# Output stores on ScalarE's DMA queue, and a new written-out order, in a fused linear-attention and SoLU kernel

## The chip, the core and the metric

The kernel runs on one core of a Trainium2 chip. The time is the device time of one execution in microseconds (us); a figure for a kernel is the median of several runs. The core has five instruction streams that matter here: TensorE (PE, with its weight loads PEld), VectorE (DVE), ScalarE (ACT), GpSimd (POOL) and SyncE (SP), which only issues DMA transfers here. Each engine carries out its instructions in the order in which the program lists them for it, and waits where an input or a buffer is not ready.

## What is computed

Two steps, of which the second takes the result of the first as its 4608 x 512 input (8 batches, 8 heads, 576 tokens of 64):

```python
def phi(x):
    proj = np.einsum('bhsd,df->bhsf', x, w_phi)
    proj = proj - np.max(np.abs(proj), axis=-1, keepdims=True)
    return np.concatenate([np.exp(proj), np.exp(-proj)], axis=-1)
q_p, k_p = (phi(q), phi(k))
kv = np.einsum('bhsf,bhsd->bhfd', k_p, v)
z = np.sum(k_p, axis=2)
num = np.einsum('bhsf,bhfd->bhsd', q_p, kv)
den = np.einsum('bhsf,bhf->bhs', q_p, z)[..., None] + 1e-06
x = (num / den)                       # to 4608 x 512
h = x @ w_in                          # 512 -> 1024
e = np.exp(h - h_max)
solu = h * e / (np.sum(e, axis=-1, keepdims=True) + 1e-09)
ln = (solu - mu) / np.sqrt(var + 1e-06) * g_ln
return (ln @ w_out)                   # 1024 -> 512
```

## The kernel before

**Attention units.** The 64 heads are worked in 16 units of four heads, each in two halves of two heads. Of a unit, PE projects keys and queries (`pjk`, `pjq`, and `pjm` for the 64 tokens in the middle that do not fill a tile of 128); DVE takes the row maxima (`m`) and subtracts them (`dk`, `dq`); ACT forms the features with exponentials (`ek` of keys, `fq` of queries). PE sums features times values into `kvT`: over full tiles of tokens (`kvT<-ek,rawv`) and over the middle ones (`kvT<-ek,vz`); the sums of the key features go into the same bank, in the first units on PE from `ek` itself (`kvT<-ek,ones` and `kvT<-ek,ones_half`), later from sums that POOL made (`kvT<-zacc,ones`). `kvT` is evicted to `kvs` and turned into `kvf`. In the first two units PE turns it (`kvt<-ident,kvs`), and queries are turned there too (`dT<-ident,dq`, and `dqm` for the middle); from the third on both go through DRAM and back (`dk<-kvs`, `kvf<-dk`; `dqd<-dq`, `pT<-dqd`). Then PE makes `den` and `num` from `fq` and `kvf`, ACT evicts them (`dn`, `E`), and POOL puts the quotient together (`xa`, `xb`).

**Token tiles.** The 4608 rows are 36 tiles of 128 (t = 0 to 35). ACT and POOL split a tile into a high part and a remainder (`mxh`, `mxl`), PE multiplies by `w_in` (`h`, 24 matmuls of 512 columns: high by high, high by low, low by high), DVE takes the maximum `nm`, ACT the exponentials `eu`, DVE the product and the statistics; `ub`, `du`, `uTs` turn the product through DRAM, ACT and POOL split it (`uhs`, `uls`), and PE multiplies by `w_out` (`o`, again 24). ACT evicts `o` times the row factor `sc` to `os` (128 x 512, 256 KB), and a transfer `out<-os` stores it. The last tile is cut into two halves of 256 columns, with 24 matmuls of 256 columns, an eviction and a store of 128 KB for each.

**The order.** Each step is an `op` with a name, an engine and a function. `SEQUENCE` is a table with the 2458 steps by number, and the program emits them in that order; since the instructions are kept in program order on their engine, the table is the order of each engine. It also decides which slot of a pool a tile gets, since freed slots are given out again in that order. The columns `cost` and `prio` of an `op` decide nothing here. In the weights' preparation at the start, `wraw` (loaded weights scaled in place), `win_h`, `w_out_h` (the high parts) and `w<-w,gcol` (weights times `g_ln`) run on ACT between the features. Nearly all instructions are recorded at one line, that of the helper that keeps the order (L260 before).

All transfers of the kernel before, the 37 stores too, are issued by SP.

Of the kernel before, what the change touches and what calls it, by code (L numbers as in the profile page):

```python
# [16 lines left out]
DM, DF = 512, 1024  # L17
# [38 lines left out]
    2, 123, 1, 124, 125, 78, 127, 126, 313, 94, 87, 85, 129, 80, 81, 95, 128, 82, 83, 99, 96, 84, 98, 136, 97,  # L56
    135, 101, 102, 138, 141, 103, 142, 104, 10, 79, 89, 130, 90, 314, 100, 92, 91, 131, 105, 86, 173, 224, 88,
    218, 4, 133, 112, 315, 132, 134, 317, 106, 107, 113, 114, 139, 108, 174, 93, 175, 11, 115, 219, 137, 316,
    110, 12, 178, 116, 109, 111, 117, 143, 222, 189, 181, 180, 182, 33, 140, 5, 118, 154, 13, 179, 318, 220,
    176, 6, 199, 119, 157, 145, 14, 120, 121, 221, 223, 156, 155, 148, 160, 190, 15, 149, 177, 162, 159, 184,  # L60
    28, 38, 150, 284, 22, 275, 122, 158, 161, 197, 34, 200, 183, 198, 191, 194, 192, 187, 193, 7, 195, 201, 225,
    164, 185, 144, 202, 167, 146, 35, 186, 226, 188, 196, 8, 227, 228, 39, 163, 205, 206, 29, 165, 147, 166,
    203, 207, 43, 285, 168, 422, 36, 3, 169, 289, 40, 286, 30, 23, 208, 288, 41, 287, 209, 249, 31, 290, 230,
    204, 213, 214, 232, 233, 236, 231, 255, 44, 381, 252, 210, 268, 151, 372, 235, 215, 234, 296, 24, 229, 291,
    251, 211, 45, 9, 46, 276, 25, 216, 212, 270, 423, 152, 254, 217, 237, 238, 32, 37, 271, 250, 240, 273, 424,
    272, 278, 153, 243, 274, 416, 277, 239, 256, 257, 253, 269, 170, 171, 244, 426, 16, 425, 259, 258, 319, 245,
    241, 42, 292, 262, 48, 49, 365, 246, 172, 279, 297, 50, 325, 427, 263, 260, 449, 242, 294, 382, 47, 264,
    320, 261, 280, 386, 417, 295, 293, 247, 326, 26, 281, 282, 265, 17, 266, 418, 283, 485, 469, 520, 51, 476,
    450, 27, 248, 419, 383, 302, 327, 420, 52, 300, 18, 303, 388, 385, 384, 323, 19, 298, 299, 53, 304, 367,
    321, 301, 267, 368, 305, 421, 369, 387, 308, 20, 21, 1808, 309, 389, 306, 374, 307, 1844, 332, 1826, 334,  # L70
    1809, 521, 72, 322, 324, 486, 329, 60, 328, 1810, 1811, 66, 63, 373, 375, 390, 330, 393, 333, 331, 69, 67,
    522, 345, 428, 370, 310, 371, 593, 336, 394, 61, 524, 1845, 68, 523, 490, 1812, 335, 339, 492, 525, 1813,
    1814, 346, 429, 399, 75, 628, 376, 379, 340, 377, 62, 337, 338, 391, 584, 347, 471, 311, 366, 378, 474, 487,
    73, 1846, 312, 392, 348, 76, 349, 351, 352, 395, 472, 341, 430, 634, 451, 350, 380, 1847, 488, 1817, 491,
    489, 353, 64, 70, 397, 1848, 405, 355, 400, 57, 401, 71, 354, 65, 1827, 54, 1849, 398, 432, 1862, 357, 396,
    55, 532, 1850, 1853, 586, 533, 406, 434, 356, 407, 408, 1828, 1829, 435, 342, 470, 585, 433, 58, 359, 358,
    437, 497, 436, 409, 1854, 475, 410, 1815, 1851, 1830, 74, 431, 473, 493, 455, 498, 594, 629, 411, 439, 438,
    630, 595, 631, 598, 478, 1855, 597, 632, 494, 596, 600, 633, 402, 403, 56, 1831, 404, 412, 360, 599, 413,
    1832, 59, 503, 77, 440, 443, 457, 456, 452, 343, 534, 361, 1818, 1856, 495, 1863, 453, 539, 635, 536, 480,
    362, 363, 414, 496, 1864, 1857, 444, 344, 504, 1852, 477, 1835, 481, 577, 479, 415, 364, 505, 1865, 538,  # L80
    441, 1858, 640, 636, 1866, 483, 482, 1867, 537, 454, 1868, 1859, 509, 459, 1860, 1819, 499, 500, 442, 458,
    637, 638, 484, 1833, 510, 511, 460, 445, 526, 1871, 639, 1820, 698, 579, 512, 461, 540, 501, 506, 1821,
    1816, 535, 446, 690, 541, 462, 463, 502, 464, 580, 447, 705, 1861, 513, 527, 1822, 582, 1872, 1823, 465,
    528, 641, 448, 514, 515, 587, 466, 530, 1869, 529, 1870, 531, 507, 553, 467, 740, 554, 696, 508, 581, 583,
    605, 601, 602, 543, 542, 516, 1824, 606, 544, 611, 588, 468, 545, 517, 665, 1873, 518, 547, 603, 546, 1880,
    604, 741, 742, 697, 555, 589, 548, 744, 556, 1881, 706, 612, 591, 707, 613, 578, 746, 519, 1836, 590, 743,
    1882, 1883, 607, 558, 557, 559, 561, 549, 710, 745, 708, 712, 592, 709, 1884, 560, 562, 700, 566, 666, 703,
    563, 617, 564, 1885, 567, 618, 1886, 565, 569, 568, 619, 642, 817, 689, 550, 1837, 1898, 609, 1934, 610,
    608, 647, 852, 1874, 1935, 1875, 1834, 648, 649, 701, 1936, 620, 1887, 752, 571, 570, 1937, 1876, 1952, 702,
    621, 753, 711, 622, 704, 572, 1938, 1889, 1939, 644, 646, 721, 717, 718, 645, 1899, 1940, 691, 853, 856,  # L90
    650, 643, 614, 1877, 615, 722, 652, 616, 667, 551, 854, 1941, 552, 671, 1900, 1901, 653, 573, 692, 1943,
    1838, 694, 651, 855, 1902, 655, 574, 754, 654, 623, 858, 1878, 1903, 857, 693, 695, 1904, 624, 1953, 1839,
    719, 656, 747, 801, 808, 1890, 575, 668, 657, 713, 714, 625, 669, 803, 659, 748, 658, 1907, 672, 720, 715,
    716, 670, 806, 626, 818, 749, 804, 750, 660, 1825, 802, 627, 822, 819, 674, 821, 1954, 673, 1840, 1888,
    1942, 723, 576, 726, 727, 724, 725, 676, 824, 864, 820, 675, 805, 1841, 661, 1842, 677, 751, 729, 807, 823,
    825, 679, 826, 678, 756, 730, 964, 680, 1891, 731, 732, 827, 681, 683, 759, 761, 1892, 865, 662, 921, 1908,
    699, 663, 757, 810, 929, 733, 760, 859, 1909, 682, 1916, 860, 777, 684, 862, 1905, 965, 861, 758, 1910,
    1893, 1955, 1894, 829, 830, 828, 685, 734, 778, 1895, 920, 735, 686, 767, 762, 1956, 863, 966, 968, 763,
    728, 664, 835, 967, 969, 687, 1944, 809, 755, 1957, 1896, 766, 764, 930, 1958, 769, 812, 765, 1959, 1961,
    889, 815, 1897, 813, 1879, 779, 736, 768, 688, 1988, 780, 783, 2024, 782, 785, 771, 1041, 1843, 737, 1989,  # L100
    1911, 1962, 1026, 1990, 1991, 816, 931, 1960, 2025, 836, 738, 1992, 1993, 1912, 772, 1994, 1997, 814, 890,
    739, 1963, 932, 2006, 781, 1913, 2026, 2027, 841, 784, 934, 1970, 790, 791, 970, 1906, 1082, 1032, 1998,
    770, 773, 866, 774, 811, 831, 786, 1964, 913, 832, 788, 837, 936, 787, 1965, 935, 1914, 1995, 2028, 789,
    933, 842, 2007, 792, 843, 838, 2029, 871, 941, 793, 844, 833, 971, 873, 891, 834, 795, 2030, 868, 794, 915,
    839, 2008, 895, 1945, 2009, 1999, 896, 845, 942, 892, 870, 893, 869, 1966, 796, 840, 916, 976, 972, 2010,
    2033, 974, 918, 917, 973, 2011, 1917, 867, 1971, 1076, 1033, 922, 775, 846, 797, 1915, 874, 1967, 2034, 872,
    776, 924, 876, 919, 923, 798, 977, 878, 879, 847, 975, 2012, 877, 1001, 875, 881, 848, 937, 1968, 938, 927,
    880, 1077, 925, 928, 939, 883, 2000, 894, 940, 897, 947, 1042, 1972, 849, 1080, 1043, 850, 1078, 2001, 1996,
    1079, 945, 884, 2013, 1002, 914, 851, 978, 885, 1003, 2015, 1973, 948, 2002, 1025, 1046, 1045, 898, 900,
    1946, 946, 980, 882, 2003, 953, 1044, 799, 949, 1974, 902, 903, 1047, 1975, 1081, 926, 899, 1048, 901, 800,  # L110
    1947, 954, 955, 904, 1976, 982, 981, 2004, 905, 907, 1979, 1027, 886, 1188, 1083, 956, 2031, 957, 1086, 943,
    887, 906, 2035, 1028, 1088, 908, 983, 944, 985, 1084, 1030, 958, 1144, 1031, 1194, 1153, 888, 979, 1948,
    909, 1007, 1004, 1918, 1949, 1919, 984, 986, 2036, 987, 1029, 1085, 1087, 2005, 1980, 1089, 1034, 1008, 910,
    1950, 911, 991, 950, 951, 988, 1137, 1090, 990, 952, 2032, 1920, 989, 959, 1113, 1005, 1051, 992, 960, 1052,
    993, 1921, 961, 1922, 995, 912, 994, 2096, 1189, 1154, 1049, 1009, 1036, 1155, 1095, 1190, 1925, 1191, 2097,
    1114, 1923, 2078, 1192, 996, 2098, 2037, 1158, 1039, 962, 1147, 1926, 1156, 1159, 2099, 2038, 1053, 963,
    1146, 1969, 1927, 997, 2016, 1300, 1951, 1115, 998, 2039, 2100, 1050, 1165, 1006, 1097, 1010, 1193, 1065,
    1040, 2014, 1157, 1037, 1014, 2101, 1015, 1057, 1160, 1012, 1054, 2017, 2042, 1058, 1091, 1059, 1060, 2040,
# [1188 lines left out]
```

## Time and profile before

| | before |
|---|---|
| median of 3 runs | 663.02 us (662.71 to 663.58) |
| the profiled execution | 664.01 us |
| its span (first to last event of the core) | 662.2 us |
| PE busy | 653.7 us, 99% of the span |
| DVE, ACT, POOL busy | 495.1, 368.9, 409.1 us (75%, 56%, 62%) |
| granted TensorE clock | 1.00 (full) in every slice |
| DMA, mean over the span | 209 GB/s, 138.45 MB |

The profiled execution is 1.8 us longer than its span, and 0.99 us longer than the median. The number of a row of a timeline is its start in the span; a timeline's time in brackets is how long the engine had stood idle before that row, and what released it. A matmul row's end is modelled and reaches into the next row, so the time that a block of matmuls takes is read from one row's start to the next one's.

### The profile page before, as it was taken

The numbers are of one execution on the slowest core, as the hardware profiler recorded it, in microseconds if no ns is written. First come the engines' busy times: TensorE is split into PE (matmuls) and PEld (weight loads), VectorE is DVE, ScalarE is ACT, GpSimd is POOL, SyncE is SP. The second block draws the span as 40 slices with busy tenths as digits, with TensorE's granted clock in tenths as the row PEclk, the third lists the DMA queues.
The fourth block names the chain that finished last, engine by engine and source line by source line (L and its number), as shares of the span: only waits on it lengthen the run. The fifth ranks groups of instructions, "written<-read, shape, count | busy, mean of one in ns | idle before, by whom it ended". The sixth has DMA issues, their size and how long they took to land.

```text
span 662.2 us, 13124 instructions
## 1 busy us (share of the span) xinstructions
PE 653.7 (99%) x4900; PEld 490.5 (74%) x4900; DVE 495.1 (75%) x750; ACT 368.9 (56%) x713; POOL 409.1 (62%) x447
## 2 busy tenths in 40 slices
PE   8999999999999999999999999999999999999997
PEld 6766767668777777777777777877677877788886
DVE  6999987788978687799968879788679665355340
ACT  4997775466564744556565665355745464324221
POOL 0239998757866546667876575856654775455342
PEclk9999999999999999999999999999999999999999
DMA  8987787887487946887667856874786544424241
GB/s 269 346 270 237 221 251 210 270 259 214 134 265 255 296 151 182 272 260 230 201 197 230 287 151 176 266 227 124 229 282 199 191 149 120 123 110 162 112 167 72
DMA packets 133296, 138.45 MB, mean 209 GB/s; under 512 B 55664, under 2 KB 106736, under 8 KB 132720
## 3 DMA queue, kind: packets, MB, share of 16 engines
q1 hardware_dynamic: 133232, 137.61, 65.9%
q8 instruction: 39, 0.64, 0.4%
q14 instruction: 25, 0.20, 0.1%
HBM read 87.10 MB, written 50.48 MB: 208 GB/s over the span
## 4 chain that ended last, share of the span: by engine, by line
PE 87%; DVE 6%; DMA 4%; issue 1%; ACT 1%; SPq 0%; ACTq 0%
PE o L260 30%; PE h L260 29%; PE kvT L260 11%; PE num L260 6%; PE pjk L260 4%; PE pjq L260 4%; PE den L260 2%; DVE m L260 2%; DVE w L260 1%; DVE dq L260 1%; DMA rawq<-in_q 1%; DVE dk L260 1%; DMA pT<-dqd 1%; PE pjm L260 1%; DMA dk<-kvs 1%
## 5 line engine op out<-in xcount | busy, mean ns | idle before, releaser
L260 POOL TENSOR_TENSOR uls<-uTs,uhs 128x1024 fp32r<-128x1024 f32 x36 | 86.6, 2410 | 61.8 <-ACT uhs L260 47.6
L260 PE MATMUL o<-w_out_h,uhs 128*128 128x512 f32 (+1 forms) x296 | 114.6, 387 | 0.0
L260 ACT ACTIVATE ek<-dk 128x512 f32<-128x512 f32 (+1 forms) x160 | 89.7, 584 | 44.1 <-DVE dk L260 39.4
L260 PE MATMUL o<-w_out_l,uhs 128*128 128x512 f32 (+1 forms) x296 | 113.6, 384 | 0.0
L260 PE MATMUL o<-w_out_h,uls 128*128 128x512 f32 (+1 forms) x296 | 113.5, 383 | 0.0
L260 PE MATMUL h<-win_h,mxh 128*128 128x512 f32 x288 | 91.2, 398 | 0.3 <-DVE dq L260 0.3
L260 DVE TENSOR_REDUCE nm<-h 128x1 f32<-128x1024 f32 x36 | 43.9, 1218 | 62.9 <-PE h L260 62.9
L260 PE MATMUL h<-win_l,mxh 128*128 128x512 f32 x288 | 88.9, 390 | 0.0
L260 PE MATMUL h<-win_h,mxl 128*128 128x512 f32 x288 | 88.8, 389 | 0.0
L260 ACT ACTIVATE fq<-pT 128x512 f32<-128x512 f32 (+1 forms) x140 | 74.5, 559 | 21.4 <-DMA pT<-dqd 13.8
L260 POOL TENSOR_TENSOR zt<-ek 128x512 f32<-128x512 f32 x52 | 68.8, 1322 | 24.4 <-ACT ek L260 22.8
L260 ACT ACTIVATE eu<-h,nm 128x1024 f32<-128x1024 f32 x36 | 40.0, 1111 | 69.3 <-DVE nm L260 60.3
L260 PEld LDWEIGHTS o<-w_out_h,uhs 128*128 128x128 f32 x296 | 55.6, 188 | 13.4 <-issue 1.6
L260 PEld LDWEIGHTS o<-w_out_h,uls 128*128 128x128 f32 x296 | 55.6, 188 | 11.0
L260 PEld LDWEIGHTS o<-w_out_l,uhs 128*128 128x128 f32 x296 | 55.6, 188 | 10.6
L260 PEld LDWEIGHTS h<-win_h,mxh 128*128 128x128 f32 x288 | 52.4, 188 | 13.9 <-issue 1.1
L260 PEld LDWEIGHTS h<-win_l,mxh 128*128 128x128 f32 x288 | 54.0, 188 | 11.5
L260 PEld LDWEIGHTS h<-win_h,mxl 128*128 128x128 f32 x288 | 54.1, 188 | 11.5
L260 PE MATMUL kvT<-ek,rawv 128*64 128x256 f32 x512 | 61.9, 384 | 0.0
L260 POOL TENSOR_TENSOR xa<-E,rb 128x576 f32<-128x576 f32 (+1 forms) x32 | 29.7, 931 | 51.9 <-DMA rb<-d 40.7
L260 DVE TENSOR_TENSOR eu<-h,eu 128x1024 f32<-128x1024 f32 x36 | 43.6, 1212 | 17.9 <-ACT eu L260 17.7
L260 PE MATMUL num<-fq,kvf 128*64 128x448 f32 (+1 forms) x304 | 56.2, 500 | 0.0
(96 smaller groups left out, 1231.9 us busy)
## 6 DMA issues: line engine op xcount, KB each, us to landing
du<-ub SPq DMA_DIRECT2D x36, 512.0 KB, 3.7
uTs<-du SPq DMA_DIRECT2D x36, 512.0 KB, 4.9
rb<-d SPq DMA_DIRECT2D x64, 144.0 KB, 4.4
dqd<-dq SPq DMA_DIRECT2D x14, 640.0 KB, 4.3
pT<-dqd SPq DMA_DIRECT2D x14, 640.0 KB, 5.8
out<-os SPq DMA_DIRECT2D x35, 256.0 KB, 3.2
rawq<-in_q SPq DMA_DIRECT2D x32, 256.0 KB, 4.7
rawk<-in_k SPq DMA_DIRECT2D x32, 256.0 KB, 4.5
```

What stands on the lines that cost most here:

```text
L260: return self.tc.keep_in_program_order(method(*args, **kwargs))
```

## The change

The stores of the output are issued by ACT (`nc.scalar.dma_start`) instead of SP, in ACT's order of steps; all other transfers stay with SP. `SEQUENCE` is another order of the same 2458 steps. No other line differs.

```diff
 SEQUENCE = (
...
-    2, 123, 1, 124, 125, 78, 127, 126, 313, 94, 87, 85, 129, 80, 81, 95, 128, 82, 83, 99, 96, 84, 98, 136, 97,
...
-    2435, 2452, 2311, 2455, 2436, 2400, 2383, 2239, 2401, 2453, 2456, 2454, 2437, 2457, 2409, 2417, 2410, 2418,
-    2419,
...
+    2433, 2428, 2434, 2435, 2436, 2382, 2418, 2437, 2383, 2419, 2451, 2446, 2452, 2453, 2454, 2455, 2456, 2457,
 )
...
     def moe_od_last(t, half):
         cs = slice(half * 256, half * 256 + 256)
-        nc.sync.dma_start(out=out[t * P : (t + 1) * P, cs], in_=M["os", t][:, cs])
+        nc.scalar.dma_start(out=out[t * P : (t + 1) * P, cs], in_=M["os", t][:, cs])
...
     def moe_od(t):
-        nc.sync.dma_start(out=out[t * P : (t + 1) * P, :], in_=M["os", t])
+        nc.scalar.dma_start(out=out[t * P : (t + 1) * P, :], in_=M["os", t])
...
-            op(n("od", hf), "sync", dma(2 * P * DM), z + 18 + hf, moe_od_last, (t, hf), [n("oe", hf)], (), [n("os")])
+            op(n("od", hf), "scalar", dma(2 * P * DM), z + 18 + hf, moe_od_last, (t, hf), [n("oe", hf)], (), [n("os")])
...
-        op(n("od"), "sync", dma(4 * P * DM), z + 19, moe_od, (t,), [n("oe")], (), [n("os")])
+        op(n("od"), "scalar", dma(4 * P * DM), z + 19, moe_od, (t,), [n("oe")], (), [n("os")])
```

Three places of the order follow, as the built kernels have it. A row is the line of the program, the operation, the tiles (output<-inputs, without numbers), the shape, and how many of them follow each other.

**First place.** PE in the second unit, from the first half's sum over full tiles on. Before:

```order
L260 MATMUL kvT<-ek,rawv 64x256 x8
L260 MATMUL pjm<-wph,rawk 128x128 x2
L260 MATMUL pjm<-wph,rawq 128x128 x2
L260 MATMUL kvT<-ek,vz 64x256 x4
L260 MATMUL kvT<-ek,ones 32x128 x16
L260 MATMUL kvT<-ek,ones_half 32x128 x4
L260 MATMUL dT<-ident,dq 128x128 x8
L260 MATMUL kvT<-ek,rawv 64x256 x8
```

Now:

```order
L259 MATMUL kvT<-ek,rawv 64x256 x8
L259 MATMUL pjm<-wph,rawk 128x128 x2
L259 MATMUL pjm<-wph,rawq 128x128 x2
L259 MATMUL kvT<-ek,vz 64x256 x4
L259 MATMUL kvT<-ek,rawv 64x256 x8
L259 MATMUL kvT<-ek,ones 32x128 x16
L259 MATMUL kvT<-ek,ones_half 32x128 x4
```

The second half's sum over full tiles, which needs all four `ek` steps of that half's keys, has moved up to stand directly behind the middle tokens. The row sums and the turns of queries that stood between them come after it; one `dT<-ident,dq 128x128 x4` stands further ahead than before.

**Second place.** PE between the third and the fourth unit: `kvT` is the first half of the fourth, `den` belongs to the third. Before:

```order
L260 MATMUL kvT<-fq,kvf 64x128 x4
L260 MATMUL num<-fq,kvf 64x448 x4
L260 MATMUL kvT<-ek,vz 64x256 x4
L260 MATMUL den<-fq,kvf 32x288 x8
L260 MATMUL kvT<-zacc,ones 32x128 x4
```

Now:

```order
L259 MATMUL kvT<-fq,kvf 64x128 x4
L259 MATMUL num<-fq,kvf 64x448 x4
L259 MATMUL kvT<-ek,vz 64x256 x4
L259 MATMUL kvT<-zacc,ones 32x128 x4
L259 MATMUL den<-fq,kvf 32x288 x8
```

The last matmuls into `kvT` have changed places with `den`. Behind both orders stand the same rows up to the first that reads the turned sums: 24 matmuls `h`, `pjm`, `pjq`, and `kvT<-ek,rawv`. On DVE the step that evicts this `kvT` to `kvs` stood behind the turn `ub<-eu` of a token tile, and now stands ahead of it.

**Third place.** ACT at the end of the program. Here the rows name what an instruction waits for as well: a count of another engine (PE, DVE, Pool, Activation), or of one of the eight counters (DMAHW0 to 7) that the transfers use in turn. Before:

```order
L260 ACTIVATE eu,sm<-h,nm 128x1024 [waits DVE_49,Pool_49]
L260 CAST uhs<-uTs 128x1024 [waits DMAHW4_49]
L260 ACTIVATE os<-o,sc 128x512 [waits DMAHW1_49,PE_49,Activation_49]
L260 CAST uhs<-uTs 128x1024 [waits DMAHW6_49,Activation_49]
L260 ACTIVATE os<-o,sc 128x512 [waits PE_49,Pool_49]
L260 ACTIVATE os<-o,sc 128x512
L260 ACTIVATE os<-o,sc 128x256 [waits DMAHW7_49,PE_49,Activation_49]
L260 ACTIVATE os<-o,sc 128x256 [waits PE_49]
L260 ACTIVATE os<-o,sc 128x512 [waits DMAHW0_49,PE_49,Pool_49]
```

Now:

```order
L259 DMA out<-os 128x512 [waits DMAHW1_49,Activation_49]
L259 CAST uhs<-uTs 128x1024 [waits DMAHW0_49,Pool_49]
L259 ACTIVATE os<-o,sc 128x512 [waits PE_49,Pool_49]
L259 ACTIVATE os<-o,sc 128x512 [waits DMAHW2_49]
L259 ACTIVATE os<-o,sc 128x512 [waits DMAHW5_49]
L259 DMA out<-os 128x512 [waits Activation_49]
L259 DMA out<-os 128x512 [waits DMAHW3_49,Activation_49]
L259 DMA out<-os 128x512 [waits Activation_49]
L259 ACTIVATE os<-o,sc 128x256 [waits DMAHW6_49,PE_49,Pool_49]
L259 DMA out<-os 128x256 [waits Activation_49]
L259 ACTIVATE os<-o,sc 128x256 [waits PE_49]
L259 DMA out<-os 128x256 [waits Activation_49]
```

Before, a whole tile of 512 columns was evicted last; now the two halves of 256 columns come last. The stores stand among ACT's own instructions, and some of them wait for a counter of the transfers as SP's do: through the program 25 of the 37 do so. Such a counter's wait holds until the transfer that used that counter before, eight transfers earlier in the program, has landed.

## Rows read from the trace of the kernel before

**Rows 1.** Busy time of each engine by stretch: length, then engine, busy us (instructions), granted clock, DMA

```profile
0.00:100.00 100.00, 95.25 (x1096) 68.40 (x1098) 91.39 (x158) 77.08 (x153) 59.71 (x57) 1.00 0.84 266
100.00:658.00 558.00, 558.00 (x3807) 422.03 (x3804) 403.69 (x593) 291.14 (x560) 349.44 (x391) 1.00 0.64 200
```

**Rows 2.** Waits of PE, whole span: releaser, us in total, times, longest

```profile
PE kvT L260 <- DMA kvf<-dk: 1.3, 1, 1.3
PE pjm L260 <- DMA rawk<-in_k: 0.9, 2, 0.6
```

**Rows 3.** Waits of SP's DMA queue, whole span

```profile
SPq L260 <- DVE kvs L260: 95.5, 26, 9.3
...
SPq L260 <- ACT os L260: 34.1, 9, 8.9
```

**Rows 4.** Store instructions on SP: ns min/median/max, first and last start

```profile
L260 SPq DMA_DIRECT2D out<-os x37: 332/424/1848, 120.1 to 659.3; - x37
```

**Rows 5.** Chain that ended last, 149 to 169 us: start, us, what

```profile
149.45 5.67 PE h L260 x24
...
162.77 5.44 PE h L260 x24
```

**Rows 6.** Timeline of PE from 35 us: start, us, instructions, idle before and releaser

```profile
35.23 0.49 PE L260 MATMUL pjm<-wph,rawk 64*128 64x128 f32 x4 [0.36 <-DMA rawk<-in_k]
...
35.87 0.66 PE L260 MATMUL kvT<-ek,vz 64*64 64x256 f32 x8
36.46 1.08 PE L260 MATMUL kvT<-ek,ones 128*32 128x128 f32 x32
...
37.69 1.09 PE L260 MATMUL dT<-ident,dq 128*128 128x128 f32 x8
...
46.07 1.18 PE L260 MATMUL den<-fq,kvf 128*32 128x288 f32 x16
```

**Rows 7.** Timeline of ACT from 31 us

```profile
31.95 1.19 ACT L260 ACTIVATE wraw<-wraw 128x1024 f32<-128x1024 f32 x1
33.03 1.14 ACT L260 ACTIVATE ek<-dk 128x512 f32<-128x512 f32 x2
...
35.12 0.98 ACT L260 COPY E<-num 128x288 f32<-128x288 f32 x3
35.98 0.65 ACT L260 ACTIVATE ek<-dk 128x512 f32<-128x512 f32 x1
...
37.62 0.64 ACT L260 ACTIVATE ek<-dk 128x512 f32<-128x512 f32 x1
```

**Rows 8.** Timeline of ACT from 45 us

```profile
45.15 2.61 ACT L260 ACTIVATE w<-w,gcol 128x512 f32<-128x512 f32 x4
```

**Rows 9.** Timeline of DVE from 89 us

```profile
89.54 0.58 DVE L260 STREAM_TRANSPOSE kvs<-kvT 128x384 f32<-128x384 f32 x1 [0.73 <-ACT E L260]
```

**Rows 10.** Timeline of SP's DMA issues from 90 us

```profile
90.52 0.52 SPq L260 DMA_DIRECT2D du<-ub  x1
```

**Rows 11.** Chain that ended last, 90 to 104 us

```profile
90.15 5.31 DMA dk<-kvs
...
95.48 4.27 DMA kvf<-dk
...
102.31 0.97 PE den L260 x16
```

**Rows 12.** Timeline of ACT from 655 us

```profile
655.76 0.48 ACT L260 ACTIVATE os<-o,sc 128x256 f32<-128x256 f32 x1 [2.36 <-PE o L260]
658.56 0.69 ACT L260 ACTIVATE os<-o,sc 128x512 f32<-128x512 f32 x1 [2.32 <-PE o L260]
```

**Rows 13.** Landing of the last store, from the view of tile os

```profile
DMA to landing us min/median/max: 2.0/2.0/2.0
```

**Rows 14.** DMA issues: KB each, median us to landing

```profile
dk<-kvs SPq DMA_DIRECT2D x28, 192.0 KB, 2.4
...
out<-os SPq DMA_DIRECT2D x2, 128.0 KB, 1.7
```

251 rows, old and new, of the table SEQUENCE are left out of this document.

## The prediction

> **What bounds the kernel now.** I read the busy times by stretch first [rows 1]. PE is busy for 558.00 of the 558.00 us between 100 and 658 us; ahead of 100 us it is busy for 95.25 of 100, and behind 658 for almost nothing. So a change of the order can take out at most the 4.75 us of idle PE at the head, and some of the tail; everywhere else it can only shuffle work that lies beside PE, or add waits to it. The clock is 1.00 throughout, so nothing is to be had there. The waits of PE say what the idle time at the head is [rows 2]: one of 1.3 us for the turned sums `kvf` coming back from DRAM, and two of 0.9 us together for loads of keys. Last I read the waits of SP, since the stores leave it [rows 3]: SP waits 34.1 us for `os` in 9 stores, the longest 8.9, and all transfers behind those stores wait with it. But the first store starts at 120.1 us [rows 4], where PE has no idle time left to give back. Moving the stores can't help the head, and behind 100 us it can help nothing on PE.
>
> **The change part by part.** *PE's own work: 0.* The steps are the same ones. A block of 24 matmuls of 512 columns takes 5.44 us, and 5.67 where PE enters it from the smaller kinds [rows 5], so an order could cost 0.23 us for each further change of kind. Counted in both orders, there are 31 stretches of `h` and `o`, and 167 changes of kind; with the durations of the trace on each row both orders come to 648 us of pure work, 0.1 apart.
>
> *First place, second unit: +0.95.* Its key sum over the second half needs the last `ek` of the unit. Before, that `ek` starts at 37.62 and takes 0.64, so it is ready at 38.26 [rows 7], while the row sums and turns from 36.46 on keep PE at work [rows 6]. Now the sum stands directly behind the middle tokens. PE reaches it at 36.46, plus 0.52 for the four turns moved ahead (half of the 1.09 for eight), so at about 36.98; less 0.36 if the wait for keys at 35.23 is covered by them [rows 6]. ACT's list up to that `ek` has lost one `wraw`, 33.03 - 31.95 = 1.08, and one `E`, (35.98 - 35.12)/3 = 0.29, and gained one `fq` of about 0.53: ready at 38.26 - 0.84 = 37.42 [rows 7]. PE waits 0.44 more than before, whether as 0.44 here, or as 0.80 here and the 0.36 gone. If ACT keeps its old pace, without the 0.84, it waits 1.3; if earlier differences favour it, nothing: 0 to 1.3. The `den` that follows moves too: on ACT two `w<-w,gcol` of 0.65 each [rows 8] and one more `wraw` stand ahead of the `fq` that it needs, which came behind it or sooner; they use up ACT's spare time there. Walked along the same rows, the last `fq` of the second `den` comes at 47.7 and PE at 47.8, a tie that any delay of ACT turns into a wait. I take 0.5, between 0 and the 1.08 of the `wraw`.
>
> *Second place, fourth unit: -1.2.* The chain is `kvs` at 89.54 [rows 9], `dk<-kvs` from 90.15 for 5.31 us, `kvf<-dk` from 95.48 for 4.27 [rows 11]; it is late by 1.3 us [rows 2]. Now the last matmuls into this `kvT` run ahead of `den` instead of behind it, so 0.97 us earlier [rows 11], while the reader of `kvf` stays where it was. `kvs` waited 0.73 us with DVE idle [rows 9], and on DVE the 1.25-long `ub` that stood ahead of it now comes behind, so DVE is free in time; and `du<-ub`, 512 KB issued at 90.52, just behind `dk<-kvs` [rows 10], comes later and no longer shares the engines with it. The median landing of `dk<-kvs` is 2.4, not 5.31 [rows 14]. 0.97 for sure would leave 0.3; with a part of the 2.9 I take -1.2, bounds 0 (another load in its way) and -1.3.
>
> *The other waits of the head: -0.3.* The two waits for keys, 0.9 us together [rows 2], now have four turns or a projection ahead of them, but what sets them is when a load lands, which the order hardly moves. Bounds 0 and -0.9; a third, since only the later one, of 0.36, is clearly covered.
>
> *The tail: -0.4.* Before, the last thing evicted is a whole tile, 0.69 us, against 0.48 for a half [rows 12]; the last store lands 2.0 us after its start [rows 13], that of a half takes 1.7 in the median [rows 14]. Now halves come last: -0.2 and -0.3, of which I take -0.4; bounds -0.2 and -0.5. PE's last 24 matmuls of 256 columns take as long as 12 of 512.
>
> *The stores on ACT: +0.2.* 37 x 0.424 = 15.7 us of issuing [rows 4] goes from SP to ACT. ACT is busy for 291.14 of 558 us there [rows 1], so 267 us of idle time hide it. If that cover were gone, ACT would be a bound and PE would see up to 15.7; at 55% busy it is not near. What could show is a wait: 25 stores carry the counter of a transfer eight places earlier, and ACT, with `eu`, `E`, `fq` or `mxh` behind the store, stands until that has landed. Laying PE's durations along the order, that transfer's place is 5 to 20 us ahead of the store; SP reaches transfers late by up to 9.3 us where it waits for `kvs` [rows 3], so a hold of some us can happen, and PE is reached only if ACT's lead is used up. I take 0.2; bounds 0 and 2.6, two waits the size of the 1.3 in [rows 2].
>
> What SP gains from the move is seen in [rows 3]: 34.1 us of standing still for `os`, more than the 15.7 of issuing. The Trainium skill ("DMA: Bandwidth & Descriptors", section "Issuing engines are not separate DMA queues") says that transfers started by several engines run on the same 16 DMA engines, and that issuing from more of them saves only the sequencer's time. By that rule the move alone is worth nothing in time and the sum without its +0.2 would be -0.95, 662.1 us; the trace agrees in so far as SP's waits reach no PE wait behind 100 us, but shows 34.1 us, not 15.7, freed on SP.
>
> The sum: 0 + 0.45 + 0.5 - 1.2 - 0.3 - 0.4 + 0.2 = -0.75, against the profiled execution's 664.01: 663.3. That execution is 0.99 above the median of the runs shown, so against the median it is 663.02 - 0.8 = 662.2 us.
>
> **The rivals.** *Slower: ACT is held by a store.* One mechanism: a store on ACT waits for the transfer that used its counter, SP comes to that transfer late, and the `eu` or `fq` behind the store reaches PE late. For it: SP's waits of up to 9.3 us [rows 3], and places with only 5 to 7 us between the two. Against it: the usual distance is 10 us or more, and PE has had no wait behind 100 us though ACT itself stood idle for 267 us. It decides when SP's lateness plus the landing exceeds the distance by more than ACT's lead. At 1.3 us each, two such places turn -0.8 into +1.8: 664.8 us.
>
> *Faster: the new order doesn't delay the head.* If ACT, whose list is shorter at the first place, is ready in time, the +0.95 is gone, and the waits go as far as they can: -1.3 - 0.9 - 0.5 = -2.7, 660.3 us. For it: the place holds less `wraw` work ahead of the key sum; against it: PE now comes to that sum at 36.6 to 37.0, ahead of the 37.69 at which it still had turns to do before [rows 6], and ACT's 0.84 doesn't reach that far.
>
> *Nothing happens:* that the second place is hidden anyway can't be, its 1.3 us stand on PE; but it may be given back one step later, at the next sum of the unit, and then the forecast's -0.8 is about 0, 663.0 us. I count this inside the forecast.
>
> **How the numbers follow.** Forecast 0.48, its own range 661.2 to 663.6; slower rival 0.26; faster rival 0.26. A measurement of this kernel tells about 0.2%, 1.3 us, from no change: faster is below 661.7, slower above 664.35. Of the forecast a quarter lies below, 0.05 above; of the faster rival nine tenths below; of the slower one seven tenths above. Faster 0.12 + 0.23 = 0.35, slower 0.02 + 0.18 = 0.20, the rest, 0.45, within. The range runs from the faster rival's 660.3, a little below for its own spread, to a little above the slower rival's 664.8: 660.2 to 665.0.
>
> **What would show it.** PE's waits in the changed profile: the one for `kvf<-dk` near 100 us gone or below 0.4; a new one for ACT `ek` between 36 and 38 us, and one for `fq` ahead of `den` near 47; PE full again from 102 us to the last matmul; the last eviction a half of 0.48 us. Among SP's waits `os` is gone, and ACT shows waits for transfers in front of its stores. The prediction is wrong if PE is idle by more than 0.5 us anywhere between 100 and 650 us (the slower rival), or if PE's idle time ahead of 100 us falls below 3 us (the faster one).

## The result and the profile after

The changed kernel takes 667.33 us (median of 15 runs, 663.44 to 671.58), the kernel before 663.44 beside it (15 runs, 662.71 to 665.15): a ratio of 1.0061, 95% interval 1.0046 to 1.0076. It is slower by 0.6%, and its runs spread three times as wide. The forecast of 662.2, range to 665.0, was wrong, and no rival named what made it slower. The profiled execution took 667.28 us, with a span of 665.5.

The busy times of the changed kernel by stretch, the answer to [rows 1] (length; then PE, PEld, DVE, ACT, POOL; granted clock, DMA share, GB/s):

```profile
0.00:100.00 100.00, 97.28 (x1100) 70.87 (x1102) 88.72 (x152) 76.94 (x153) 59.24 (x56) 1.00 0.84 273
100.00:300.00 200.00, 200.00 (x1532) 147.68 (x1530) 164.38 (x256) 116.78 (x235) 137.63 (x155) 1.00 0.73 224
300.00:400.00 100.00, 99.56 (x736) 74.51 (x733) 84.47 (x127) 57.99 (x113) 65.11 (x68) 1.00 0.71 223
400.00:500.00 100.00, 96.28 (x699) 71.52 (x698) 84.26 (x118) 54.35 (x107) 63.51 (x67) 1.00 0.66 202
500.00:660.00 160.00, 160.00 (x828) 126.61 (x828) 78.79 (x102) 62.77 (x108) 84.52 (x104) 1.00 0.46 147
```

The head has less idle time than before (2.72 us against 4.75), but between 300 and 500 us PE now stands still for 0.44 + 3.72 us, where before it never did. PE's waits name the places, the answer to [rows 2]:

```profile
PE pjq L259 <- issue: 2.3, 1, 2.3
PE den L259 <- DVE qz L259: 1.5, 2, 1.0
...
PE dT L259 <- DVE dq L259: 0.7, 1, 0.7
PE dT L259 <- DVE dqm L259: 0.6, 1, 0.6
PE o L259 <- ACT E L259: 0.4, 1, 0.4
```

The waits for `kvf` and for keys are gone; `qz` is new. It is a step of the later units (from the second half of the fifth on): ACT and then DVE scale the query features by their sums, so that `den` is a plain sum over `qz`. The DVE step in the view of that tile, first before, then after: ns min/median/max, first and last start.

```profile
L260 DVE SCALAR_TENSOR_TENSOR qz<-fq,kvf,qz x46: 777/819/2733, 145.7 to 558.6; 128x576 f32<-128x576 f32 x46
```

```profile
L259 DVE SCALAR_TENSOR_TENSOR qz<-fq,kvf,qz x46: 771/819/6078, 143.2 to 565.5; 128x576 f32<-128x576 f32 x46
```

One instruction of the same shape takes 0.82 us or 6.08. The timelines of the changed kernel around it, DVE, POOL and PE, show when:

```profile
403.18 1.21 DVE L259 TENSOR_REDUCE nm<-h 128x1 f32<-128x1024 f32 x1
404.31 7.28 DVE L259 SCALAR_TENSOR_TENSOR qz<-fq,kvf,qz 128x576 f32<-128x576 f32 x2
411.52 1.27 DVE L259 BATCH_NORM_STATS2 bst<-eu 128x6 f32<-128x512 f32 x2
...
414.17 1.28 DVE L259 TENSOR_TENSOR dk<-pjk,m 128x512 f32<-128x512 f32 x2
```

```profile
403.42 1.28 POOL L259 TENSOR_TENSOR zacc<-zacc,ek 64x512 f32<-64x512 f32 x1
404.67 0.32 POOL L259 TENSOR_TENSOR xa<-E,rb 128x64 f32<-128x64 f32 x1
404.95 1.26 POOL L259 TENSOR_TENSOR xb<-E,rb 128x512 f32<-128x512 f32 x1
406.18 2.35 POOL L259 TENSOR_TENSOR uls<-uTs,uhs 128x1024 fp32r<-128x1024 f32 x1
408.50 1.27 POOL L259 TENSOR_TENSOR zt<-ek 128x512 f32<-128x512 f32 x1
409.85 1.13 POOL L259 TENSOR_TENSOR zacc<-zt 128x256 f32<-128x256 f32 x1
```

```profile
411.74 0.69 PE L259 MATMUL den<-qz,ones 128*32 128x288 f32 x8 [1.01 <-DVE qz L259]
412.23 0.43 PE L259 MATMUL kvT<-zacc,ones 128*32 128x128 f32 x8
414.96 1.16 PE L259 MATMUL pjq<-wph,rawq 64*128 64x128 f32 x16 [2.30 <-issue]
...
417.42 0.50 PE L259 MATMUL o<-w_out_h,uhs 128*128 128x512 f32 x1 [0.41 <-ACT E L259]
```

The rows show five POOL instructions without a gap from 403.42 to 409.77, and the first gap, 0.08 us, ahead of the second `zacc`, which has to wait for `zt`. The first of the two `qz` ends 0.62 us behind the start of that gap (6.08 us after 404.31, at 410.39), and the `zacc` that follows the gap is itself longer than usual (1.13 us; 0.74 at 402.61). Everything behind `qz` on DVE is then late: PE stands still for 1.01 us ahead of `den`, and for 2.30 ahead of `pjq`, which starts at 414.96. For `pjq` the profile names no releaser; that it waits for the first half of `dk<-pjk`, which ends at about 414.8, is inferred from the times. Near 329 us another `qz`, of 4.60 us, stands beside `xa`, `pm` and `uls`, up to POOL's next gap, ahead of `sa`:

```profile
329.17 4.60 DVE L259 SCALAR_TENSOR_TENSOR qz<-fq,kvf,qz 128x576 f32<-128x576 f32 x1
```

```profile
330.80 2.35 POOL L259 TENSOR_TENSOR uls<-uTs,uhs 128x1024 fp32r<-128x1024 f32 x1
333.24 0.58 POOL L259 TENSOR_SCALAR sa<-sm 128x1 f32<-128x1 f32 x1
```

It costs PE 0.44 us by the view of waits, 1.1 against the usual length of that step.

### The profile page after: what moved, and what is told of

The parts are those of the page before. It is cut to its first block, busy times and chain, and to the rows that moved or that the text cites. A ratio compares the mean times of both kernels' runs of the same rounds, so it can differ in the third digit from the quotient of the medians.

```text
span 665.5 us, 13139 instructions
## 1 busy us (share of the span) xinstructions
PE 655.5 (98%) x4900; PEld 493.4 (74%) x4900; DVE 500.6 (75%) x750; ACT 369.4 (56%) x713; POOL 410.0 (62%) x447
## 4 chain that ended last, share of the span: by engine, by line
PE 86%; DVE 11%; issue 1%; DMA 1%; ACT 0%; DVEq 0%
PE h L259 29%; PE o L259 28%; PE kvT L259 11%; PE num L259 6%; PE pjq L259 4%; PE pjk L259 4%; DVE m L259 3%; PE den L259 3%; DVE qz L259 2%; DVE dq L259 2%; DVE dk L259 2%; DVE w L259 1%; PE pjm L259 1%; DMA wraw<-in_w_in 1%; PE warm L259 0%
## 5 line engine op out<-in xcount | busy, mean ns | idle before, releaser
L259 DVE SCALAR_TENSOR_TENSOR qz<-fq,kvf,qz 128x576 f32<-128x576 f32 x46 | 54.7, 1206 | 7.2 <-ACT qz L259 7.0
L259 ACT ACTIVATE qz<-fq,kvf 128x576 f32<-128x576 f32 x46 | 34.4, 771 | 41.3 <-DMA kvf<-dk 39.4
```

The lines of the kernel that those rows point to most:

```text
L259: return self.tc.keep_in_program_order(method(*args, **kwargs))
```

## The experiments

All were measured beside the kernel before (663.3 to 663.5 in each series). Theory A is that DVE's `qz` waits for a gap in POOL's work, and that the new order puts unbroken POOL runs beside it; theory B that the stores hold ACT. Of each edit the main lines are shown, and "..." stands for what is left out.

**Only the stores, only the order.** The kernel before, with its old table, and the stores on ACT (the two halves of the last tile likewise):

```diff
-        nc.sync.dma_start(out=out[t * P : (t + 1) * P, :], in_=M["os", t])
+        nc.scalar.dma_start(out=out[t * P : (t + 1) * P, :], in_=M["os", t])
```

> The old order, only the 37 stores issued by ACT. Theory A (the order does it: DVE's qz step stands still while POOL runs one TENSOR_TENSOR behind the other, 6.08 us instead of 0.82 in the changed kernel's trace): as before, 662.8 to 664.2 us, and the longest qz at most 3 us. Theory B (the stores on ACT do it, by holding ACT): 665 to 669 us, with PE idle behind 100 us and ACT waiting for a store there.

The changed kernel, with its new table, and the stores on SP:

```diff
-        nc.scalar.dma_start(out=out[t * P : (t + 1) * P, :], in_=M["os", t])
+        nc.sync.dma_start(out=out[t * P : (t + 1) * P, :], in_=M["os", t])
```

> The new order, all transfers issued by SP. Theory A: slow as the changed kernel, 665 to 669 us in the median and spread over several us, with a qz of over 4 us in the trace. Theory B: the spread is gone and the head's gain is left, about 662.4 us.

The old order with ACT's stores takes 664.99 us, ratio 1.0034 (1.0022 to 1.0047); its longest `qz` is 2.73. The new order with SP's stores takes 670.25, ratio 1.0103 (1.009 to 1.0117): more than theory A's 669, and its four runs lie within 1 us. So the new order is the slow part, and ACT's stores are worth 2.9 us in it; in the old order they cost 1.5, between the two theories. Part of that is seen in its trace: behind 100 us PE waits 1.6 us for `kvf` (1.3 before) and, new, for `mxl`:

```profile
208.10 0.73 PE L260 MATMUL h<-win_h,mxl 128*128 128x512 f32 x2 [1.07 <-POOL mxl L260]
```

The rows of ACT, then of POOL, ahead of it:

```profile
203.62 0.53 ACT L260 COPY E<-num 128x448 f32<-128x448 f32 x1 [2.53 <-PE num L260]
203.65 0.82 ACTq L260 DMA_DIRECT2D out<-os  x2
```

```profile
206.78 1.27 POOL L260 TENSOR_TENSOR mxl<-xa,mxh 128x512 fp32r<-128x512 f32 x1 [4.36 <-ACT mxh L260]
```

The two stores stand on ACT behind `E`, which waited 2.53 us for PE. `os` and `mxl` take their buffers from the same pool, and POOL also waits for the semaphore of the second of these stores: issued at 204.03, it landed 2.6 us later, at 206.65, just ahead of `mxl`. The `mxh` that the profile names ended at about the same time; which of the two held `mxl` is read from this closeness, not tested.

**The gap in POOL's work.** A small POOL instruction behind each `xa`, `xb`, `mxl` and `uls`:

```diff
+    brk = work.tile([P, 1], F32, tag="brk", bufs=1, name="brk")
+    def pool_break(made):
+        nc.gpsimd.tensor_scalar(out=brk, in0=made, scalar1=1.0, scalar2=None, op0=ALU.mult)
...
             nc.gpsimd.tensor_tensor(out=dst, in0=e[:, cs], in1=rb[:, cs], op=ALU.mult)
+            pool_break(dst[:, :1])
...
```

> The changed kernel with a small POOL instruction (128 x 1) behind each xa, xb, mxl and uls step, which reads that step's result and so waits for it: a gap in POOL's work. POOL gets about 120 x 0.27 = 32 us more work. Theory A: qz gets its turn in the gaps, none above 3.5 us, PE idle behind 100 us below 0.7 us, 662.0 to 663.5 us and less spread. Theory B: unchanged, 665 to 669 us.

664.38 us, ratio 1.0018 (1.0009 to 1.0027), runs from 663.77 to 665.1; the longest `qz` is 2.25 us. 3 us of the loss and most of the spread are gone although POOL does 29 us more (439.4 busy). The expected 662.0 to 663.5 was missed: PE has new waits, the longest of 0.88 us for `uls`, at 111 us. Then only at the two places, five instructions in all:

```diff
             nc.gpsimd.tensor_tensor(out=dst, in0=e[:, cs], in1=rb[:, cs], op=ALU.mult)
+            if (st["u"], sub) in ((8, 1), (10, 1)):
+                pool_break(dst[:, :1])
...
         hi_lo_sub(nc.gpsimd, lo, full, hi)
+        if t in (9, 20):
+            pool_break(M["ul", t].bitcast(F32)[:, 0, :1])
```

> The changed kernel with small POOL instructions (128 x 1, each reads the step before it and so waits for it) at two places only: behind the xa and xb steps and the uls of the two unbroken POOL runs that lay beside the long qz of 4.60 and 6.08 us. Five small instructions in all. Theory A (qz waits for a gap in POOL's work, and these two places are where it reaches PE): most of the loss of 3.9 us goes, 662.5 to 664.5 us, and no qz over 3 us at 329 or 404 us. If many places share the loss: still 666 us or more.

662.06 us (12 runs), ratio 0.9984 (0.9973 to 0.9995): 5.3 us less than the changed kernel, and the only version with ACT's stores that beats the one before. The timelines of POOL and DVE at the second place:

```profile
403.02 0.83 POOL L259 TENSOR_TENSOR xa<-E,rb 128x64 f32<-128x64 f32 x1
403.94 0.62 POOL L259 TENSOR_SCALAR brk<-xa 128x1 f32<-128x1 f32 x1
...
405.89 0.21 POOL L259 TENSOR_SCALAR brk<-xb 128x1 f32<-128x1 f32 x1
```

```profile
402.67 1.80 DVE L259 SCALAR_TENSOR_TENSOR qz<-fq,kvf,qz 128x576 f32<-128x576 f32 x2
```

Both `qz` are through after 1.80 us instead of 7.28, and it is POOL that waits: `xa` takes 0.83 instead of 0.32, and `brk` 0.62, where the next one takes 0.21. Between the rows of PE in this trace and in the changed kernel's, the distance grows by 1.1 us at the first place and by about 4 at the second, and hardly anywhere else behind 100 us. PE is full:

```profile
100.00:655.00 555.00, 555.00 (x3786) 420.10 (x3783) 402.49 (x598) 291.26 (x560) 351.32 (x396) 1.00 0.64 199
```

With the instructions at the second place alone:

```diff
-            if (st["u"], sub) in ((8, 1), (10, 1)):
+            if (st["u"], sub) in ((10, 1),):
...
-        if t in (9, 20):
+        if t == 20:
```

> The changed kernel with the small POOL instructions at the second place only (behind xa, xb and the uls near 404 us; three instead of five). In the changed kernel's trace that place cost PE 4.0 us and the first, near 329 us, 1.1. So the long qz of 4.6 near 329 stays, 662.5 to 663.8 us, and the upper part of the spread (over 666) is gone. If the two share the loss evenly: 664.5 or more.

663.83 us, ratio 1.0009 (1.0 to 1.0017); the `qz` of 4.60 near 328 us stays. So the second place is worth 3.5 us and the first 1.8, against about 4 and 1.1 in the one trace; with the changed kernel's spread these medians are good to about 2 us.

**What about `qz` waits.** One SBUF tensor as input instead of two; the addition of the first half of the features is left out:

```diff
-        nc.vector.scalar_tensor_tensor(
-            out=g, in0=st["qf", sub, 1][:, j], scalar=z_of(st, sub, 1, j), in1=g, op0=ALU.mult, op1=ALU.add
-        )
+        nc.vector.tensor_scalar(out=g, in0=st["qf", sub, 1][:, j], scalar1=z_of(st, sub, 1, j), scalar2=None, op0=ALU.mult)
```

> The changed kernel with the DVE step of qz reading one SBUF tensor instead of two: it multiplies the second half of the query features by its sums and leaves out the addition of the first half, so the denominators lack that half. Theory A in its narrow form (it is the second SBUF input that makes DVE wait for POOL): qz constant at about 0.7 us beside any POOL run, PE full behind 100 us, 662.3 to 663.3 us. Theory A in a wide form (any DVE instruction of SBUF operands waits for POOL): long qz of over 3 us remain, 665 to 669 us. A rival, that DVE's place in the order is late and not qz itself: 665 us or more with short qz.

667.47 us, ratio 1.0054 (1.0036 to 1.0073), as slow as the changed kernel. The tile view of `qz`:

```profile
L259 DVE TENSOR_SCALAR qz<-fq,kvf x46: 472/520/5778, 142.6 to 564.6; 128x576 f32<-128x576 f32 x46
```

So the second input is not needed for the wait. The wide form is too wide as well: the 36 DVE transposes `ub`, which also go from SBUF to SBUF, take 1.19 to 1.25 us in both kernels, also where POOL works beside them (the one at 328.01 in the changed kernel, beside `zacc`). The same trace shows what the stall costs afterwards (stretches as above; the granted clock is the third number from the right):

```profile
412.00:413.00 1.00, 0.00 (x0) 0.00 (x0) 1.00 (x3) 0.00 (x0) 1.00 (x1) 1.00 0.00 0
413.00:414.00 1.00, 0.83 (x8) 0.86 (x10) 1.00 (x3) 0.00 (x0) 0.83 (x3) 0.64 0.00 0
414.00:415.00 1.00, 1.00 (x14) 1.00 (x13) 1.00 (x2) 0.00 (x0) 0.82 (x3) 0.50 0.07 16
415.00:416.00 1.00, 1.00 (x13) 1.00 (x13) 0.96 (x3) 0.68 (x2) 0.00 (x0) 0.50 0.00 0
416.00:417.00 1.00, 1.00 (x10) 0.80 (x8) 1.00 (x2) 1.00 (x3) 0.00 (x0) 0.65 0.54 198
417.00:418.00 1.00, 1.00 (x5) 0.81 (x5) 0.91 (x2) 1.00 (x4) 0.00 (x0) 1.00 0.08 4
```

PE idles for 2.3 us up to 413.17, the clock still at 1.00, and then runs near half clock (0.50, that is 1.2 GHz) for some 3 us.

**Longer POOL runs.** Four small instructions (128 x 32) without a wait between them, ahead of the `uls` of both places:

```diff
+    def pool_more():
+        for i in range(4):
+            cs = slice(32 * i, 32 * i + 32)
+            nc.gpsimd.tensor_tensor(out=more[:, cs], in0=win_l[:, i, :32].bitcast(F32), in1=win_l[:, i, 32:64].bitcast(F32), op=ALU.add)
...
+        if (st["u"], sub) in ((8, 1), (10, 1)):
+            pool_more()
```

> The changed kernel with each of the two POOL runs made longer by four small independent instructions (128 x 32, about 0.2 us each, 0.8 us a run). Theory A: both long qz get longer by 0.8 us, to about 5.4 and 6.9, and PE waits that much more: 0.8 to 1.6 us on top of the changed kernel's 667.3, so 668 to 669 in the median. If qz does not wait for POOL: 667.3, since POOL has spare time.

This missed its 668 to 669: 665.71 us, less than the changed kernel's 667.33, ratio 1.0035 (1.001 to 1.006). Its 12 runs fall into two groups, six from 662.3 to 664.2 and six from 667.2 to 669.6, and in the profiled execution (663.04) the longest `qz` is 2.53. In it `qz` got through right behind `xa` at the first place and behind `xb` at the second, while the first small instruction there was stretched, to 0.76 us from 0.24, and POOL had no gap. So small POOL instructions in a row can let DVE in, why is not shown, and the added length is not what was tested. For theory A the run says only that the two outcomes of the same program differ by some 5 us.

**Head and tail by themselves.** The new order for its first 672 steps (PE until 150 us), the old for the rest, stores on SP; then with the last 128 steps from the new order too. The kernels have the tables written out; in short, with the names OLD and NEW for the two:

```python
HEAD = NEW[:672] + [i for i in OLD if i not in NEW[:672]]
SEQUENCE = HEAD                                                       # the first
SEQUENCE = HEAD[:2330] + [i for i in NEW if i not in HEAD[:2330]]     # the second
```

> The new order for its first 672 steps (PE until about 150 us), the old order for all the rest, stores on SP. Both theories: the head's part by itself. The trace of the changed kernel reaches 216 us of the program 1.0 us earlier than before; so 662.4 us, 661.8 to 663.2, and no spread. If the new head costs nothing and gains nothing, 663.4.

> The new order for its first 672 steps, the old one up to step 2330, the new one for the last 128, which evict and store the halves last; all stores on SP. Against the kernel with the new head alone (662.96): the eviction is 0.2 us and the last store 0.3 us shorter, 662.3 to 662.8 us, 0.1% to 0.2% faster than before. If the tail is hidden or SP comes late to the last stores: 663 us or more.

662.96 us for the head (ratio 0.9995, 0.9983 to 1.0006), 662.51 with the tail (0.9987, 0.9978 to 0.9996). The medians give 0.56 us for the head and a further 0.45 for the tail, but the head's interval holds no change at all, and the 0.45 stands between two series; only the two together are clear of noise.

**The stores again, with `qz` out of the way.** The kernel with the five small instructions, stores on SP:

> The new order with the five small POOL instructions at the two places (662.06 with the stores on ACT), but all stores issued by SP. If SP, standing at a store, makes a later load late in this order (in the run with the new order and the stores on SP, two stores took SP 7.8 us and a load of queries behind them came 2.4 us late for PE, which then ran at half clock for some us): 664 to 666 us, with that wait near 395 us. If the 2.9 us between the two new-order kernels came only from other meetings of qz and POOL: 662.1, within 0.7.

666.07 us, ratio 1.0039 (1.0026 to 1.0051), against 662.06 with the stores on ACT: 4.0 us. SP's issues, then PE, in its trace:

```profile
382.70 8.27 SPq L259 DMA_DIRECT2D out<-os  x2
...
391.77 0.40 SPq L259 DMA_DIRECT2D rawq<-in_q  x1
```

```profile
395.42 2.08 PE L259 MATMUL pjq<-wph,rawq 64*128 64x128 f32 x16 [2.67 <-DMA rawq<-in_q]
```

Two stores take 8.27 us of SP's time, 7.6 of them waiting for the eviction of the second (the view of SP's waits names `E`, which stands right behind that eviction on ACT), and the load of queries behind them starts at 391.77. In the changed kernel SP's row is:

```profile
382.90 0.40 SPq L259 DMA_DIRECT2D rawq<-in_q  x1
```

9 us earlier. What it costs PE is the distance from `den` to the next `h`, first with the stores on SP, then with those on ACT:

```profile
392.08 0.67 PE L259 MATMUL den<-qz,ones 128*32 128x288 f32 x8
...
399.23 0.72 PE L259 MATMUL h<-win_h,mxh 128*128 128x512 f32 x2
```

```profile
389.39 0.67 PE L259 MATMUL den<-qz,ones 128*32 128x288 f32 x8
...
392.42 0.73 PE L259 MATMUL h<-win_h,mxh 128*128 128x512 f32 x2
```

That is 7.15 us against 3.03: 4.1 us, of which 2.67 are the wait and most of the rest the projections at half clock (2.08 us for 16 that take 1.16 at full clock). The profiled execution, 668.57, is the slowest of the five; the other 2.5 us that it loses lie ahead of 70 us, before the first store (140.3), so they have another cause.

## Why the prediction was wrong

**The step that failed** is the carrying over of [rows 1]: that PE has no wait behind 100 us in the old order was taken for a property of the kernel, and the sum had, for all that lies behind 100 us, only the term "the stores on ACT", +0.2. In its place the runs showed 5.3 us for two meetings of `qz` with POOL, shown by the five small instructions that undo them (667.33 to 662.06). With them undone the kernel is 1.3 us faster than the one before, not far from the forecast's 0.8, though not term by term, as below. The trace of the kernel before held a warning: the same DVE instruction between 777 and 2733 ns, with nothing in its own shape to explain it. An order that leaves PE's rows as they were can still move POOL's rows against DVE's, and I compared the orders engine by engine, not two engines against each other.

**PE's own work, 0:** right. With the two meetings undone PE is full from 100 to 655 us and busy for 653.8 us, against 653.7 before; the span is 660.0.

**First place, +0.95:** wrong in kind. PE goes from `kvT<-ek,vz` to the moved sum without a wait (37.01 and 37.60), since it comes 0.6 us later than I walked it: two turns of queries, at 8.16 and 12.81 us, had waited for DVE, 0.7 and 0.6 us. ACT's last `ek` is done at 37.20. `den` starts at 46.58 without a wait, 0.51 later than in [rows 6].

**Second place, -1.2:** right. Timeline of PE after, the first reader of that `kvf`:

```profile
97.03 1.95 PE L259 MATMUL kvT<-ek,rawv 128*64 128x256 f32 x16
98.81 1.67 PE L259 MATMUL num<-fq,kvf 128*64 128x448 f32 x8
```

No wait is left, and PE is there 0.98 us before the 99.79 of the kernel before.

**The head as a whole:** the terms add up to -0.55 and the head alone measured -0.56, but that is luck: the first place's waits are not those of the forecast, the new waits for DVE at 8 and 13 us stand in no term, and the interval of the measurement is wider than the sum. PE's idle time ahead of 100 us, 2.72, is also below the 3 us that were to show the faster rival, and ACT was ready in time as that rival had it; its 2.7 us did not come: once `den` and `kvT` of the second place are through, PE is 1.0 us ahead (102.17 against 103.21).

**The tail, -0.4:** right in kind. The last eviction is a half, and the last store lands 1.7 us after its start; the tail alone measured -0.45, which is not clear of noise.

```profile
662.41 0.47 ACT L259 ACTIVATE os<-o,sc 128x256 f32<-128x256 f32 x1 [2.35 <-PE o L259]
662.92 0.34 ACTq L259 DMA_DIRECT2D out<-os  x1
```

**The stores on ACT, +0.2, and "can help nothing on PE":** wrong on both sides. In the new order they save 4.0 us, because there SP's standing at a store does reach PE; in the old order they cost 1.5. The value of the move hangs on what stands behind the store on either engine. The Trainium skill ("DMA: Bandwidth & Descriptors", section "Issuing engines are not separate DMA queues") says that initiating transfers on another engine saves only the sequencer's time for that, which is usually small beside the transfer. The runs differ from it: two stores took 8.27 us of SP's time, most of it waiting, and moving the stores was worth 4.0 us. **The slower rival**, ACT held by a store until a transfer has landed, did not decide in the changed kernel, though its sign, PE idle by more than 0.5 us behind 100 us, appeared: ACT stands once for the landing of a store, 3.0 us ahead of `mxh`, and none of PE's waits names a store. Its relative, a store that keeps a buffer too long, is the 1.07 of the old order with ACT's stores.

Open stays why one execution of the changed kernel takes 663.44 us and another 671.58. In its one trace the two meetings cost 5 us, and its runs with a mean granted clock of 0.997 or less are all above 667 us; the trace with one input has that mean, from its one stretch at half clock. Whether the shorter executions escape a meeting was not traced.

## What to carry to other kernels

Before an order is changed, look for instructions whose duration varies at one shape: they wait while they run, no view of waits names them, and a new order can turn 2.7 us into 6.1. Where one engine's step needs gaps in another's work, see what breaks that other's run: here five instructions that wait for the step before them, 0.2 to 0.6 us each on POOL, were worth 5.3 us. And an issuing engine works its transfers off in order, as SP did here: price a moved transfer by what stands behind it there and here.

## What the hardware showed

DVE's `qz` (two SBUF inputs, or one) did not run beside POOL's `TENSOR_TENSOR`: it lasted through the rest of one and four more in a row (6.08 us) and ran in the first gap, and POOL's next instruction was then longer (1.13 us instead of 0.74). All twelve traces bear this out. In them there are 98 `qz` of over 1.45 us, and every one ends 0.61 to 0.62 us (0.32 in the form with one input) after some POOL instruction ended. In 93 of them POOL pauses there, for 0.07 us or more; in the other five the next POOL instruction follows without a pause and is stretched. The Trainium skill ("SBUF — State Buffer", section "SBUF: two separate sides") says that VectorE and GpSimd share a port pair under an exclusive lock, which a VectorE instruction takes if it has two SBUF inputs or runs in a 2-port mode, and that the one that starts first blocks the other for its whole instruction. The traces agree on the exclusion in both directions; that the form with one input waits as well would fall under the second case, which no run here tells apart. They differ in that `qz`, at the long meetings, did not get its turn when the POOL instruction then running ended, but several instructions later, in most cases where POOL paused: 6.08 us, though the `zacc` beside which it began had 0.39 us to go. Why POOL's pause, or in five cases something else, lets it in is not shown.

A PE that stood still for 2.3 us came back at half clock for some 3 us in one trace, and kept its full clock (1.00) after a pause of the same length in another (the changed kernel's at 414.96). So the same stall has two prices; what decides between them is not shown.
